# Placing VectorE sums one by one behind residual additions, and a score tile of its own for the last remainder product

## The chip, the cores and the metric

One core of a Trainium2 chip. The metric is the device time of one execution in microseconds (us), median of several runs. Five engines work side by side: TensorE (PE in the profile, PEld for its weight loads), VectorE (DVE), ScalarE (ACT), GpSimd (POOL) and SyncE (SP).

## The reference, cut to what matters

An attention with a relative bias for 8 batches of 576 tokens and 8 heads of 64, then a mixer: a low-rank product over the tokens with a residual, and a two-layer network with a residual.

```python
scores = scale * (q @ k.T) + bias            # per batch and head
x = softmax(scores) @ v                      # -> [8, 576, 512]
h = x.transpose(0, 2, 1) @ U @ V             # U [576, 32], V [32, 576]
u = x + h.transpose(0, 2, 1)
out = u + maximum(u @ w_ch1, 0.0) @ w_ch2    # w_ch1 [512, 2048], w_ch2 [2048, 512]
```

## The kernel before

The network's rows are handled in nine chunks of 512 rows: chunks 0 to 7 are the first 512 tokens of each batch, chunk 8 ("the last chunk", the remainder) the last 64 tokens of all batches. Chunks 7 and 8 are computed as a pair, with sums of their transposed tokens (fold_u), and the second matrix product of a chunk is cut into 2 x 2 blocks with seven products in place of eight. This takes sums of "inner rows" beforehand (low_sum, high_sums, last_sum) and additions of partial results afterwards (add with the residual u, and more). All of these sums and additions run on VectorE, in one queue.

This is the second product, with the cuts marked. `x`, `z` and `y` are three accumulators, each one PSUM bank; each `product` is 16 matmuls of 128 x 256 on TensorE. `y_first` is true for chunk 7 only, and only chunk 7 passes a `between` that does something: it places the sums for chunk 8.

```python
        x = bank()
        yield from product(x, "a11", "b11", True)
        add(x, blk(0, 0), u_of(j, 0, 0))
        z = bank()
        yield from product(z, "s3", "t3", True)
        add(z, blk(1, 1), u_of(j, 1, 1))
        if y_first:
            y = bank()
            yield from product(y, "a12", "b21", True)
            more(y, 0, 0)
        yield from product(x, "s2", "t2")
        add(x, blk(1, 0), u_of(j, 1, 0))
        for i in range(2):
            rows.last_sum(i)
        yield from product(z, "a22", "t4")
        more(z, 1, 0)
        between()
        yield from product(x, "s1", "t1")
        more(x, 1, 1)
        store(j, 1, ob[1])
        between()
        # ... (other chunks do product y here; chunk 8 does half of it)
        between()
        yield from product(x, "s2", "b22")
        add(x, blk(0, 1), u_of(j, 0, 1))
        # ... (stores)
```

A product may write into an accumulator again only after the addition behind the product before it has read the accumulator. This is the end of the program, where the last pair of heads is mixed while chunk 6's second product runs; PE takes chunk 6's matmuls between these calls, and all the rest after `work.finish()`:

```python
    work.run(0.5)
    hm = ps_s.tile([128, 2, 512], FP32, name="sc")
    mix_h(g, hm[:, 0, :])              # 4 matmuls, then addition u_tok on VectorE
    mix_rem(g, hm[:, 1, 0:128])()      # 1 matmul, then addition u_rem on VectorE
    fold_u(1, slice(0, 2))             # the four sums of transposed tokens
    for i in (2, 3, 4):
        fold_u(i, slice(0, 1))
    ready[B - 1] = ready[B] = True
    work.finish()
```

The softmax here doesn't subtract the row's maximum and nothing guards it: scores larger than these inputs give would overflow.

Of the kernel before, what the change touches and what calls it, by code (L numbers as in the profile page):

```python
# [12 lines left out]
FP32 = mybir.dt.float32  # L13
# [23 lines left out]
def kernel(  # L37
# [40 lines left out]
    ps_s = ctx.enter_context(  # L78
        tc.tile_pool(name="ps_s", bufs=2, space=bass.MemoryType.PSUM)
    )  # L80
# [343 lines left out]
    def add(ps, o, u):  # L424
        split = lambda x: x.rearrange("p t (a c) -> p t a c", c=128)
        nc.vector.tensor_tensor(out=split(o), in0=split(ps), in1=u, op=ALU.add)  # L426

    def u_of(j, i, h):
        t, a = slice(2 * i, 2 * i + 2), slice(2 * h, 2 * h + 2)
        if j < B:  # L430
            return u_tok[j % 3][:, a, t, :].rearrange("p a t c -> p t a c")
        return u_rem[:, t, a, :]
# [95 lines left out]
        yield from first_product(j, tail, g, sums)  # L528
        yield from second_product(j, rows)

    def second_product(j, rows, between=lambda: None, y_first=False):
        ob = [osb.tile([128, 2, DM], FP32, name="ob") for _ in range(2)]
        left = {
            "a11": lambda n: rows.lo[:, n, 0:256],
            "a12": lambda n: rows.hi[:, n, 0:256],
            "a22": lambda n: rows.hi[:, n, 256:512],
            "s1": lambda n: rows.s1[n // 4][:, n % 4, :],
            "s2": lambda n: rows.s2[n // 4][:, n % 4, :],
            "s3": lambda n: rows.s3[:, n, :],
        }  # L540
        right = {
            "b11": lambda n: w2b[:, n, 0:256],
            "b21": lambda n: w2b[:, 8 + n, 0:256],
            "b22": lambda n: w2b[:, 8 + n, 256:512],
            "t1": lambda n: tw[0][:, n, :],
            "t2": lambda n: tw[1][:, n, :],
            "t3": lambda n: w2b[:, n, 256:512],
            "t4": lambda n: tw[2][:, n, :],
        }

        def bank():
            return acc().rearrange("p (t c) -> p t c", t=2)

        def half(ps, a, b, t, first):
            for n in range(8):
                nc.tensor.matmul(  # L556
                    ps,
                    lhsT=left[a](n)[:, t * 128 : t * 128 + 128],
                    rhs=right[b](n),
                    start=first and n == 0,  # L560
                    stop=n == 7,
                    skip_group_check=True,
                )
                yield HALF

        def product(ps, a, b, first=False):
            for t in range(2):
                yield from half(ps[:, t, :], a, b, t, first and t == 0)

        def blk(i, h, t=slice(0, 2)):  # L570
            return ob[i][:, t, 256 * h : 256 * h + 256]

        def more(ps, i, h, t=slice(0, 2)):
            o = blk(i, h, t)
            nc.vector.tensor_tensor(out=o, in0=ps, in1=o, op=ALU.add)  # L575

        def late(t):
            y = acc()[:, 0:256].rearrange("p (t c) -> p t c", t=1)
            yield from half(y[:, 0, :], "a12", "b21", t, True)
            more(y, 0, 0, slice(t, t + 1))  # L580
            store_rem(0, ob[0], slice(t, t + 1), slice(0, 256))
# [6 lines that stand above are left out]
        add(z, blk(1, 1), u_of(j, 1, 1))  # L588
        if y_first:
            y = bank()  # L590
            yield from product(y, "a12", "b21", True)
            more(y, 0, 0)
        yield from product(x, "s2", "t2")
        add(x, blk(1, 0), u_of(j, 1, 0))
        for i in range(2):
            rows.last_sum(i)
        yield from product(z, "a22", "t4")
        more(z, 1, 0)
        between()
        yield from product(x, "s1", "t1")  # L600
        more(x, 1, 1)
        store(j, 1, ob[1])
        between()
        if j < B:
            if not y_first:
                y = bank()
                yield from product(y, "a12", "b21", True)
                more(y, 0, 0)
        else:
            store_rem(1, ob[1])  # L610
            yield from late(0)
        between()
        yield from product(x, "s2", "b22")
        add(x, blk(0, 1), u_of(j, 0, 1))
        if j < B:
            store(j, 0, ob[0])
        else:
            store_rem(0, ob[0], cols=slice(256, 512))
            yield from late(1)
# [25 lines left out]
    def fold_u(i, ks):  # L645
        o = slice(ks.start, ks.stop)
        b1, b2 = slice(ks.start, ks.stop), slice(2 + ks.start, 2 + ks.stop)
        t1, t2 = t12[:, b1, :], t12[:, b2, :]
        out_, x, y = (
            (t1, pb8[:, b1, :], pb7[:, b1, :]),  # L650
            (t2, pb8[:, b2, :], t1),
            (t34[:, b1, :], pb8[:, b2, :], pb8[:, b1, :]),
            (t34[:, b2, :], pb7[:, b2, :], t2),
        )[i - 1]
        nc.vector.tensor_tensor(out=out_, in0=x, in1=y, op=ALU.subtract)
# [8 lines left out]
    def pair_chunk(sixth):  # L664
# [5 lines left out]
        rows8 = Rows(  # L670
            *[t[:, 0:4096].rearrange("p (n c) -> p n c", c=S0) for t in flat],
            [], [],
            v_bf[0].rearrange("p k h c -> p (k h c)").bitcast(FP16)[
                :, 0:2048
            ].rearrange("p (n c) -> p n c", c=256),
        )
# [103 lines left out]
        todo8 = [lambda i=i: relu_act(rows8.hi[:, 2 * i : 2 * i + 2, :])  # L780
                 for i in range(4)]
        sums8 = [lambda i=i: rows8.low_sum(i) for i in range(2)]
        sums8 += [lambda i=i: rows8.high_sums(i) for i in range(2)]

        def between():
            while todo8:
                todo8.pop(0)()
            for _ in range(2):
                if sums8:
                    sums8.pop(0)()  # L790

        rest = second_product(B - 1, rows7, between, True)
        for p in range(67):
            if p in turns:
                f, n = turns[p]
# [297 lines left out]
    def mix_h(g, hm=None):  # L1093
        b, pr = divmod(g, NPAIR)
        x, tt = x_pr[g], tt_pr[g]
        if hm is None:
            hm = acc()
        for t in range(4):
            nc.tensor.matmul(  # L1099
                hm[:, t * 128 : (t + 1) * 128],  # L1100
                lhsT=vpad[:, t * 128 : (t + 1) * 128],
                rhs=tt,
                start=(t == 0),
                stop=(t == 3),
                skip_group_check=True,
            )
        nc.vector.tensor_tensor(  # L1107
            out=u_tok[b % 3][:, pr, :, :],
            in0=hm.rearrange("p (t c) -> p t c", t=4),
            in1=x[:, 0:4, :],  # L1110
            op=ALU.add,
        )
        if on_pe(g):
            return
        nc.sync.dma_start_transpose(
            out=uT[b % 3][:, pr, :].rearrange("c (t p) -> c t p", p=128),
            in_=u_tok[b % 3][:, pr, :, :].rearrange("p t c -> p (t c)"),
        )
# [23 lines left out]
    def mix_rem(g, hr):  # L1142
        b, pr = divmod(g, NPAIR)
        x, tt = x_pr[g], tt_pr[g]
        v0 = S0 - 64 if b % 2 else S0
        nc.tensor.matmul(hr, lhsT=vpad[:, v0 : v0 + 128], rhs=tt, start=True, stop=True)  # L1146
        rows = slice(64 * (b % 2), 64 * (b % 2) + 64)

        def post():
            nc.vector.tensor_tensor(  # L1150
                out=u_rem[rows, b // 2, pr, :],
                in0=hr[rows, :],
                in1=x[rows, 4, :],
                op=ALU.add,
            )
            if b % 2 == 0:
                return
            r = b // 2
            if b < B - 1:
                if pr < NPAIR - 1:  # L1160
                    return
                prs = slice(0, NPAIR)
            elif pr == 0:
                return
            else:
                prs = slice(0 if pr == 1 else pr, pr + 1)
            nc.sync.dma_start_transpose(
                out=uT_rem[:, prs, r * 128 : (r + 1) * 128],
                in_=u_rem[:, r, prs].rearrange("p a c -> p (a c)"),
            )  # L1170

        return post

    work = Work()
# [186 lines left out]
    for g in range(NPAIR, NG):  # L1361
        b, pr = divmod(g, NPAIR)
        for seg in range(3):
# [7 lines left out]
            if seg == 1:  # L1371
                n = 0
# [47 lines left out]
    def last_rem(g):  # L1420
        hr = ps_s.tile([128, 2, 512], FP32, name="sc")
        mix_rem(g, hr[:, 0, 0:128])()
# [14 lines left out]
    work.run(0.7)  # L1437
    turn(g)
    work.run(0.5)
    hm = ps_s.tile([128, 2, 512], FP32, name="sc")  # L1440
    mix_h(g, hm[:, 0, :])
    mix_rem(g, hm[:, 1, 0:128])()
    fold_u(1, slice(0, 2))
    for i in (2, 3, 4):
        fold_u(i, slice(0, 1))
    ready[B - 1] = ready[B] = True
# [31 lines left out]
```

## Time and profile before

| | before |
|---|---|
| median of 3 runs | 395.13 us (395.12 to 395.38) |
| profiled execution | 394.26 us, span 392.5 us |
| PE busy | 374.7 us, 95% of the span |
| VectorE busy | 313.0 us, 80% |
| waits of PE after 326 us | 0.78, 0.99 and 0.89 us |

The order of reading is: which engine is full, in which stretch it is not, and what the engine waited for in that stretch. From 326 us on PE is full but for the three waits, so they are all that a change of VectorE's order can win there. One thing about sizes: the profile models the end of a matmul, so an idle time of PE starts late. Of the wait before 373.95 us the profile shows 0.89 us, but the group before it started at 371.15 us and 16 matmuls take 1.745 us of PE's stream, so PE could have gone on at 372.90 us: 1.05 us. The difference, 0.16 to 0.17 us here and at the other waits, is what the profile adds to the last matmul of a group (1.91 - 1.745 us). The Trainium skill, "TensorE: Matmul & The Clock Gate", Single matmul latency, gives a single warm matmul (398 + N)/2.4 ns, 166 ns more than its N columns; the profile's ends agree with that, but since they are modelled this is no measurement of the array. I therefore compare starts.

### The profile page before, as it was taken

How to read it: one execution, taken by the hardware profiler on the slowest of the kernel's cores; microseconds unless marked ns; L12 is line 12 of the kernel's file. 1: busy time of each engine (PE TensorE's matmuls, PEld its weight loads, DVE VectorE, ACT ScalarE, POOL GpSimd, SP SyncE). 2: the span in 40 equal slices, each digit the busy share in tenths (PEclk: the TensorE clock that was granted, in tenths of full speed). 3: DMA queues.
4: the chain of work that ended last, by engine and by line, in shares of the span. 5: the costliest groups of instructions: out<-in, count | busy, mean ns of one | idle time of the engine just before them, and what ended most of it. 6: DMA issues, size and time to landing. Idle time of an engine off the chain costs nothing.

```text
span 392.5 us, 10256 instructions
## 1 busy us (share of the span) xinstructions
PE 374.7 (95%) x4145; PEld 249.4 (64%) x4145; DVE 313.0 (80%) x692; ACT 222.6 (57%) x338; POOL 129.0 (33%) x187
## 2 busy tenths in 40 slices
PE   7799999999999999999999999999999998999995
PEld 6366555565578656875588556865587467645874
DVE  7866898879898678878787788888997788678873
ACT  5987555555655676556655665556456650488400
POOL 4999817553454055405540543131000000000000
PEclk9999999999999999999999999999999999999999
DMA  7999999999999799959998999979003001200023
GB/s 135 170 106 170 166 203 109 165 72 183 154 74 107 161 126 90 81 145 139 111 70 134 134 126 68 92 182 133 17 16 116 21 8 35 109 0 2 0 109 107
DMA packets 163542, 40.66 MB, mean 104 GB/s; under 512 B 151632, under 2 KB 159096, under 8 KB 163496
## 3 DMA queue, kind: packets, MB, share of 16 engines
q0 software_dynamic: 110304, 18.24, 65.9%
q1 hardware_dynamic: 51928, 20.86, 25.2%
q10 hardware_dynamic: 1264, 0.92, 1.0%
q8 instruction: 32, 0.52, 0.6%
q14 instruction: 14, 0.11, 0.1%
HBM read 37.84 MB, written 9.45 MB: 120 GB/s over the span
## 4 chain that ended last, share of the span: by engine, by line
PE 84%; DVE 11%; ACT 2%; issue 1%; POOL 0%; DVEq 0%; POOLq 0%; ACTq 0%
PE acc L556 24%; PE acc L410 22%; PE o L1025 11%; PE sc L931 8%; PE acc L696 4%; PE acc L462 3%; DVE g L421 2%; PE sc L696 2%; PE acc L1099 2%; PE sc L949 2%; PE sc L970 1%; DVE p_sb L1001 1%; PE o L1183 1%; PE acc L905 1%; DVE qkT L874 1%
## 5 line engine op out<-in xcount | busy, mean ns | idle before, releaser
L940 ACT ACTIVATE p_sb<-sc 128x1024 bf16<-128x1024 f32 (+1 forms) x125 | 120.2, 1015 | 95.0 <-PE sc L931 95.0
L410 PE MATMUL acc<-uT,w1b 128*128 128x512 f16 x448 | 106.6, 380 | 1.2 <-ACT g L419 0.7
L410 PEld LDWEIGHTS <-w1b 128*128 128x128 f16 x448 | 40.5, 98 | 53.8 <-issue 13.9
L1001 DVE TENSOR_TENSOR p_sb<-p_sb,eb 128x768 bf16<-128x768 bf16 (+4 forms) x156 | 65.6, 454 | 0.6 <-ACT p_sb L940 0.4
L421 DVE TENSOR_SCALAR g<-acc 128x512 f16<-128x512 f32 x78 | 52.2, 684 | 7.9 <-PE acc L410 6.8
L1025 PEld LDWEIGHTS <-p_sb 128*128 128x128 bf16 x1550 | 53.4, 97 | 4.7 <-issue 0.9
L1025 PE MATMUL o<-v_bf,p_sb 128*128 128x65 bf16 x1475 | 55.6, 193 | 0.2 <-DVE xp L1051 0.2
L931 PE MATMUL sc<-qkT 64*128 64x512 bf16 x256 | 40.2, 382 | 1.5 <-ACT p_sb L940 0.9
L1381 POOL COPY gate<-xp 1x2 bf16<-1x2 bf16 x18 | 3.5, 193 | 112.7 <-DVE xp L1051 112.7
L556 PEld LDWEIGHTS <-g 128*128 128x128 f16 x336 | 32.1, 98 | 10.3 <-issue 5.4
L556 PEld LDWEIGHTS <-stage 128*128 128x128 f16 x336 | 32.1, 98 | 7.6 <-issue 3.4
L1051 DVE TENSOR_TENSOR xp<-o,rcp 128x320 bf16<-128x320 f32 x60 | 29.5, 492 | 3.2
L556 PE MATMUL acc<-w2b,g 128*128 128x256 f16 x224 | 28.1, 273 | 0.6 <-DVE g L421 0.6
L275 POOL DMA_DIRECT2D v_bf<-in_v_dram x32 | 28.5, 917 | 0.4 <-issue 0.3
L556 PE MATMUL acc<-tw,stage 128*128 128x256 f16 x224 | 28.1, 273 | 0.0
L419 ACT ACTIVATE g<-acc 128x512 f16<-128x512 f32 x34 | 20.4, 599 | 11.0 <-PE acc L410 10.8
L426 DVE TENSOR_TENSOR ob<-acc,u_tok 128x512 f32<-128x512 f32 x28 | 19.2, 688 | 9.2 <-PE acc L556 8.8
L1107 DVE TENSOR_TENSOR u_tok<-acc,xp 128x512 f16<-128x512 f32 x31 | 21.3, 687 | 6.2 <-PE acc L1099 6.0
L575 DVE TENSOR_TENSOR ob<-acc,ob 128x512 f32<-128x512 f32 (+1 forms) x25 | 16.7, 666 | 9.2 <-PE acc L556 8.9
L981 ACT ACTIVATE p_sb<-sc 128x640 bf16<-128x640 f32 x31 | 21.6, 698 | 0.3 <-PE sc L973 0.3
L962 ACT ACTIVATE p_sb<-sc 128x512 bf16<-128x512 f32 x31 | 18.5, 597 | 4.6 <-PE sc L1146 1.0
L275 POOL DMA_DIRECT2D qb<-in_k_dram x20 | 18.2, 910 | 1.6 <-issue 1.6
(168 smaller groups left out, 571.0 us busy)
## 6 DMA issues: line engine op xcount, KB each, us to landing
out_dram<-ob SPq DMA_DIRECT2D x16, 512.0 KB, 3.3
v_bf<-in_v_dram POOLq DMA_DIRECT2D x32, 128.0 KB, 5.9
qb<-in_q_dram POOLq DMA_DIRECT2D x23, 128.0 KB, 4.1
qb<-in_k_dram POOLq DMA_DIRECT2D x23, 128.0 KB, 4.2
w1b<-in_moe_w_ch_dram POOLq DMA_DIRECT2D x4, 512.0 KB, 6.6
w2b<-in_moe_w_ch_dram POOLq DMA_DIRECT2D x2, 1024.0 KB, 14.3
qb<-in_q_dram POOLq DMA_DIRECT2D x10, 64.0 KB, 5.3
qb<-in_k_dram POOLq DMA_DIRECT2D x10, 64.0 KB, 4.2
```

What stands on the lines that cost most here:

```text
L275: nc.gpsimd.dma_start(out=dst, in_=src[b, :, t * 128 : (t + 1) * 128, :].rearrange("h p d -> p h d"),)
L410: nc.tensor.matmul(gp_, lhsT=w1b[:, ct, nt * 128 : (nt + 1) * 128], rhs=rhs[:, ct, :], start=(ct == 0), stop=(ct == 3),)
L421: nc.vector.tensor_relu(out=g[:, nt, :], in_=gp_)
L556: nc.tensor.matmul(ps, lhsT=left[a](n)[:, t * 128 : t * 128 + 128], rhs=right[b](n), start=first and n == 0, stop=n == 7, skip_group_check ...
L696: nc.tensor.matmul(ps, lhsT=lhs, rhs=rhs[:, kt, :], start=first and kt == 0, stop=kt == 1, skip_group_check=True,)
L931: nc.tensor.matmul(sp[:, hh, :], lhsT=kT[rows, i * 128 : (i + 1) * 128], rhs=qT[rows, 0:S0], start=True, stop=True,)
L940: nc.scalar.activation(P[:, i, hh, 0:S0], sp[:, hh, :], AF.Exp, scale=scale)
L981: nc.scalar.activation(P4[:, 0:SP], sp.rearrange("p a c -> p (a c)")[:, 0:SP], AF.Exp, scale=scale,)
L1001: nc.vector.tensor_tensor(out=t, in0=t, in1=e, op=ALU.mult)
L1025: nc.tensor.matmul(o[:, qt * 66 : qt * 66 + 65], lhsT=lhs[:, c0 : c0 + 128], rhs=rhs, start=(kt == NKT and qt == 0), stop=(kt == NKT - 1), ...
L1051: nc.vector.tensor_tensor(out=xo[:, :, hh], in0=o[:, :, 0:64], in1=rbc, op=ALU.mult)
L1107: nc.vector.tensor_tensor(out=u_tok[b % 3][:, pr, :, :], in0=hm.rearrange("p (t c) -> p t c", t=4), in1=x[:, 0:4, :], op=ALU.add,)
```

## The change

The intent was to take all three waits of PE. The remainder product of the last pair of heads gets its own score tile; the token sums go behind residual additions of chunk 6; the sums of chunk 8's inner rows are placed one by one between chunk 7's additions instead of two (or four) at a time.

```diff
--- before.py
+++ after.py
@@ -528,7 +528,7 @@
         yield from first_product(j, tail, g, sums)
         yield from second_product(j, rows)
 
-    def second_product(j, rows, between=lambda: None, y_first=False):
+    def second_product(j, rows, between=lambda n: None, y_first=False):
         ob = [osb.tile([128, 2, DM], FP32, name="ob") for _ in range(2)]
         left = {
             "a11": lambda n: rows.lo[:, n, 0:256],
@@ -588,19 +588,21 @@
         add(z, blk(1, 1), u_of(j, 1, 1))
         if y_first:
             y = bank()
+            between(1)
             yield from product(y, "a12", "b21", True)
             more(y, 0, 0)
+            between(1)
         yield from product(x, "s2", "t2")
         add(x, blk(1, 0), u_of(j, 1, 0))
         for i in range(2):
             rows.last_sum(i)
         yield from product(z, "a22", "t4")
         more(z, 1, 0)
-        between()
+        between(1)
         yield from product(x, "s1", "t1")
         more(x, 1, 1)
         store(j, 1, ob[1])
-        between()
+        between(1)
         if j < B:
             if not y_first:
                 y = bank()
@@ -609,9 +611,9 @@
         else:
             store_rem(1, ob[1])
             yield from late(0)
-        between()
         yield from product(x, "s2", "b22")
         add(x, blk(0, 1), u_of(j, 0, 1))
+        between(6)
         if j < B:
             store(j, 0, ob[0])
         else:
@@ -780,12 +782,13 @@
         todo8 = [lambda i=i: relu_act(rows8.hi[:, 2 * i : 2 * i + 2, :])
                  for i in range(4)]
         sums8 = [lambda i=i: rows8.low_sum(i) for i in range(2)]
-        sums8 += [lambda i=i: rows8.high_sums(i) for i in range(2)]
-
-        def between():
+        sums8 += [lambda i=i, w=w: rows8.high_sums(i, (w,))
+                  for i in range(2) for w in range(2)]
+
+        def between(n):
             while todo8:
                 todo8.pop(0)()
-            for _ in range(2):
+            for _ in range(n):
                 if sums8:
                     sums8.pop(0)()
 
@@ -1437,10 +1440,11 @@
     work.run(0.7)
     turn(g)
     work.run(0.5)
-    hm = ps_s.tile([128, 2, 512], FP32, name="sc")
-    mix_h(g, hm[:, 0, :])
-    mix_rem(g, hm[:, 1, 0:128])()
+    mix_h(g, ps_s.tile([128, 2, 512], FP32, name="sc")[:, 0, :])
+    last_rem(g)
+    work.run(2.5)
     fold_u(1, slice(0, 2))
+    work.run(1.7)
     for i in (2, 3, 4):
         fold_u(i, slice(0, 1))
     ready[B - 1] = ready[B] = True
```

## The prediction

> **What bounds the kernel now.** I read the page first, then a table of busy times by stretch of the end of the run, because the compiled instruction streams of the two kernels agree on every engine until about 327 us: the matrix stream (PE) has the same 8292 rows in the same order and differs only in one output tile; ScalarE, GpSimd and SyncE keep their order; VectorE has the same operations, of which fourteen move. Nothing before 327 us can change.
>
> ```profile
> PE 374.7 (95%) x4145; PEld 249.4 (64%) x4145; DVE 313.0 (80%) x692; ACT 222.6 (57%) x338; POOL 129.0 (33%) x187
> ```
>
> PE is busy 95%. It is the bound, so only a gap of PE is worth anything. The table by stretch (columns: stretch, length, then PE, PEld, DVE, ACT, POOL busy, clock, DMA) says where gaps are:
>
> ```profile
> 326.90:331.00 4.10, 2.32 (x21) 1.90 (x20) 3.61 (x8) 0.00 (x0) 0.00 (x0) 1.00 0.18 40
> 331.00:336.10 5.10, 5.10 (x48) 4.56 (x48) 3.04 (x5) 0.00 (x0) 0.00 (x0) 1.00 0.01 3
> 336.10:361.10 25.00, 24.96 (x124) 11.97 (x123) 19.71 (x33) 18.43 (x32) 0.00 (x0) 1.00 0.11 43
> 361.10:373.90 12.80, 11.96 (x103) 9.97 (x102) 10.63 (x19) 5.92 (x7) 0.00 (x0) 1.00 0.00 0
> 373.90:388.20 14.30, 14.20 (x128) 12.41 (x127) 8.87 (x15) 0.00 (x0) 0.00 (x0) 1.00 0.30 99
> ```
>
> After 326.9 PE is short by 4.10 - 2.32 = 1.78 us in the first stretch and 12.80 - 11.96 = 0.84 us in the fourth; elsewhere it is full. The timeline of PE and of VectorE names both gaps (columns: start, duration, engine, line, operation, count, idle before and its releaser):
>
> ```profile
> 326.56 0.39 PE L1099 MATMUL sc<-tt,vpad 128*128 128x128 bf16 x4
> 327.73 0.22 PE L1146 MATMUL sc<-tt,vpad 128*128 128x128 bf16 x1 [0.78 <-DVE u_tok L1107]
> 328.00 1.91 PE L556 MATMUL acc<-tw,stage 128*128 128x256 f16 x16
> 330.91 1.91 PE L556 MATMUL acc<-tw,g 128*128 128x256 f16 x16 [0.99 <-DVE ob L426]
> ...
> 326.99 0.69 DVE L1107 TENSOR_TENSOR u_tok<-sc,xp 128x512 f16<-128x512 f32 x1 [0.91 <-PE sc L1099]
> 327.98 0.29 DVE L1150 TENSOR_TENSOR u_rem<-sc,xp 64x128 f16<-64x128 f32 x1 [0.31 <-PE sc L1146]
> 328.31 1.15 DVE L655 TENSOR_TENSOR uT<-uT_rem,uT 128x1024 f16<-128x1024 f16 x2
> 330.16 1.29 DVE L426 TENSOR_TENSOR ob<-acc,u_tok 128x512 f32<-128x512 f32 x2
> ```
>
> Gap A, 0.78 us: the remainder product (L1146) shares a score tile with the main mixing product (L1099) and waits until VectorE has read that one. Gap B, 0.99 us: the product that overwrites accumulator z waits for the residual addition z (L426 at 330.16), which stands in VectorE's queue behind the four sums of transposed tokens (L655). Gap C, 0.89 us, is in the second product of chunk 7:
>
> ```profile
> 372.01 1.28 DVE L491 TENSOR_TENSOR v_bf<-p_sb 128x1024 f16<-128x1024 f16 x2
> 373.21 0.68 DVE L575 TENSOR_TENSOR ob<-acc,ob 128x512 f32<-128x512 f32 x1
> 373.95 1.91 PE L556 MATMUL acc<-w2b,qkT 128*128 128x256 f16 x16 [0.89 <-DVE ob L575]
> ```
>
> The matmul at 373.95 may write accumulator x only once the addition at 373.21 has read it, and that came after two sums of the last chunk's rows.
>
> **What the skill says.** Trainium skill, "PSUM — Partial Sum Buffer", PSUM bank collisions raise a hardware error: guard PSUM by bank, not by address. The code's tile is 128 x 2 x 512 FP32, two banks, and the two products lie in different ones; so gap A is the tile-wise dependency, not a bank in use, and a separate tile may remove it. Same page, Engine vs sequencer instructions: VectorE's queue is strict first in, first out. The trace agrees: L426 at 330.16 runs behind L655 although its matmuls were done long before. Trainium skill, "VectorE: DVE Perf Modes", The perf-mode tier table: a two-tensor operation has a 2x mode for 16-bit SBUF operands, 1x with PSUM. The trace agrees: 128x1024 f16 in SBUF and 128x512 from PSUM both take about 0.69 us, so every moved sum costs as much as an addition.
>
> **Part 1, own score tile.** PE's four mixing matmuls are 0.055 us apart (0.22 us in the chain of waits), so the remainder product can start at 326.56 + 0.22 = 326.78, the last two z matmuls at 326.84 and 326.95, and the 16 of x (s2 by t2) at 327.06 instead of 328.00: 0.94 us.
>
> **Part 2, token sums behind the additions.** From 327.06 the 16 matmuls, 1.745 us (334.40 - 332.65, 0.109 each), end their turn at 328.80. They are followed by the z product, which needs addition z. VectorE: u_tok 326.99 to 327.68, u_rem from 327.70, addition z from 328.03 to 328.72, released 0.06 us later: 328.78. So PE is just not held, and starts at 328.80 instead of 330.91: 2.11 us won so far, 0.94 of it from part 1.
>
> Then I follow the moved sums, since they only change place. Addition x waits for its matmuls (a 16-matmul group ends 1.91 us after its start): 329.01. Two row sums, 0.60 apart, from 329.62; first token sum 330.9 to 331.6; "more z" 331.6 to 332.3; three token sums 0.34 apart, 332.28 to 333.38; "more x" 333.41 to 334.10. PE meanwhile runs s1 by t1 from 330.55, y from 332.29, and at 334.03 wants x again: a **new wait** of about 0.13 us, to 334.16. In the kernel before this matmul started at 336.14. Net of parts 1 and 2: 336.14 - 334.16 = 1.98 us.
>
> **Part 3, inner rows' sums one by one.** After: addition z 367.07, low sum 367.67, "more y" 368.28, low sum 368.88, addition x 369.60 (bound by its matmuls, as before), two row sums to 371.5, "more z" 371.41, one high sum 372.01 to 372.69. VectorE is then free when s1 by t1 ends, 371.15 + 1.91 = 373.06. "More x" starts at 373.10 instead of 373.21. PE follows 0.74 us after that start, as before (373.95 - 373.21): 373.84. **Gain 0.11 us, not 0.89**: the addition itself depends on the matmuls right before it, and product y that could fill the time has been moved ahead (y_first). The last three high sums then end near 377.7, and PE needs them at about 379.1; no new wait. The last store of chunk 7 is issued 0.7 us earlier, which only eases the output buffer's wait at 380.06, hidden anyway.
>
> Sum: 1.98 + 0.11 = 2.09 us. From 331 us PE is full apart from gap C, so an earlier start passes to the end; the final additions and stores shift with it. Predicted: 395.13 - 2.09 = **393.0 us**, 0.53%.
>
> **Rivals.** (1) *The backlog moves into the next wait*: sums postponed on VectorE hold "more x" longer than 0.13 us. For it: VectorE is busy 3.61 of 4.10 us in that stretch, and "more x" has no slack in my count. Against it: VectorE idled over 2 us between 332.65 and 336.34 in the kernel before. Each 0.1 us of error in a VectorE spacing shows fully; at worst half of B comes back, 393.6. (2) *Gap C closes wholly*, giving 0.78 us more: 392.3. For it speaks the order of the queue; against it the dependency just shown: 0.68 us of addition plus 0.10 of hand-over cannot overlap. (3) *Transposes bound*: the transposes of chunk 7 by SyncE (issued at 327.70 and 329.00) become the wait when PE arrives 2 us earlier. The median from issue to landing is 3.3 and 2.8 us, so they land near 331.0 and 331.8, needed at 334.3 and 335: hidden. If not, up to 1 us is lost: 394. (4) *Nothing*: hidden behind other work. Against it: PE has no other bound in those 61 us.
>
> **Range and chances.** The spread of the before-times is 0.26 us. Rival 1 or 3 gives up to 394, rival 2 down to 392.3. Range 392.5 to 393.9. The total of all three gaps is 2.66 us or 0.7%, so faster by over 2% is ruled out, and slower by 2% would need 8 us of new waits.
>
> **What would show it.** Right: no wait of L1146's counterpart on u_tok; PE's first matmul on z after the token products without a wait on L426's; first s2-by-b22 matmul of chunk 6 with a wait near 0.1 us on "more x"; the same matmul of chunk 7 still with 0.7 to 0.8 us of wait; span near 390.4. Wrong: a wait above 0.3 us on "more x" in chunk 6, one on a transpose at the first pair products, or a chunk-7 wait near zero.

## The result, and the profile after

The changed kernel took 392.70 us (392.12 to 393.53, 4 runs) against 395.12 us (394.30 to 395.38, 4 runs). The ratio is 0.9944, 95% interval 0.9917 to 0.9971, so it is faster, clear of the noise. A ratio here is the mean time of one kernel's runs over that of the other's of the same rounds, so not quite the ratio of the medians.

Line numbers of the changed kernel are 2 or 3 higher after the edit: L1102, L1149, L1110, L1153, L657 and L698 are L1099, L1146, L1107, L1150, L655 and L696 of before. First the table of busy times by stretch of the changed kernel, with the stretches cut at the first mixing matmul, at the first matmul of s2 by b22 in chunk 6 and in chunk 7, and at the last addition (columns as in the prediction):

```profile
327.77:335.25 7.48, 7.48 (x73) 6.73 (x71) 6.38 (x12) 0.00 (x0) 0.00 (x0) 1.00 0.11 24
335.25:372.95 37.70, 36.88 (x226) 21.91 (x224) 30.99 (x52) 24.36 (x39) 0.00 (x0) 1.00 0.08 28
372.95:387.19 14.24, 14.20 (x128) 12.42 (x127) 8.12 (x13) 0.00 (x0) 0.00 (x0) 1.00 0.31 99
```

PE is now full in the first stretch (7.48 of 7.48 us); what is left is in the second, 0.82 us. The timeline of PE in the changed kernel shows both places:

```profile
327.77 0.39 PE L1102 MATMUL sc<-tt,vpad 128*128 128x128 bf16 x4
327.99 0.22 PE L1149 MATMUL sc<-tt,vpad 128*128 128x128 bf16 x1
328.26 1.91 PE L556 MATMUL acc<-tw,stage 128*128 128x256 f16 x16
330.01 1.91 PE L556 MATMUL acc<-tw,g 128*128 128x256 f16 x16
335.25 0.27 PE L556 MATMUL acc<-w2b,stage 128*128 128x256 f16 x1
...
370.26 1.91 PE L556 MATMUL acc<-tw,qkT 128*128 128x256 f16 x16
372.95 1.91 PE L556 MATMUL acc<-w2b,qkT 128*128 128x256 f16 x16 [0.78 <-DVE ob L575]
```

The remainder product (L1149) starts 0.22 us after the mixing product, the product on z (330.01) waits for nothing, and so does the first s2-by-b22 matmul of chunk 6 (335.25). The same matmul of chunk 7 still waits 0.78 us, where it was 0.89. VectorE's timeline of the changed kernel says why:

```profile
329.24 0.69 DVE L426 TENSOR_TENSOR ob<-acc,u_tok 128x512 f32<-128x512 f32 x1
332.02 0.68 DVE L657 TENSOR_TENSOR uT<-uT_rem,uT 128x1024 f16<-128x1024 f16 x1
334.23 0.68 DVE L575 TENSOR_TENSOR ob<-acc,ob 128x512 f32<-128x512 f32 x1
...
371.12 0.68 DVE L503 TENSOR_TENSOR stage<-p_sb,p_sb 128x1024 f16<-128x1024 f16 x1
372.21 0.69 DVE L575 TENSOR_TENSOR ob<-acc,ob 128x512 f32<-128x512 f32 x1 [0.40 <-PE acc L556]
```

Addition z (329.24) now comes before the first token sum (332.02). "More x" of chunk 6 ends at 334.91 us, 0.34 us before PE needs it. In chunk 7, VectorE was free and waited 0.40 us for PE before "more x" (372.21): the wait is no longer VectorE's queue, but the addition itself.

The time comes from three stretches, measured between starts:

| | before | after |
|---|---|---|
| A: first mixing matmul to first s2-by-b22 matmul, chunk 6 | 9.58 | 7.48 |
| B: start of s1 by t1 to start of s2 by b22, chunk 7 | 2.80 | 2.69 |
| C: first mixing matmul to start of the last VectorE addition | 61.63 | 59.42 |

So 2.10 + 0.11 = 2.21 us were won in all. The spans of the two profiled executions differ by only 1.0 us, because the profiled execution of the changed kernel reached the first mixing matmul 1.21 us later (327.77 against 326.56), in code that the change doesn't touch. This is the row from 15 to 25 us of the table by stretch of the changed kernel, and then of the kernel before (the third number from the right is the granted clock):

```profile
15.00:25.00 10.00, 8.12 (x104) 5.22 (x104) 7.18 (x21) 8.60 (x12) 9.35 (x15) 0.83 1.60 132
```

```profile
15.00:25.00 10.00, 8.03 (x135) 5.36 (x132) 6.88 (x21) 9.19 (x13) 9.35 (x15) 1.00 1.69 137
```

The clock fell to a mean of 0.83 in one and not in the other, at nearly the same busy time of PE. The traces of the experiments fit this: the four with 0.83 in this row (the changed kernel twice, e1_tile, e5b_split) reach the first mixing matmul at 327.54 to 327.77 us, the six with 1.00 and no late weights (see e2_late) at 326.25 to 327.00 us. It does not go by the code: e5_split and e5b_split are one program, with 1.00 and with 0.83. Executions of the kernel before seem to fall into it too: of eleven runs, the three with a granted clock of 0.996 took 395.37 to 395.65 us, the eight with 0.998 or more 393.86 to 395.28 us. It is not the only thing that varies: in another call one of its runs took 395.67 us at 0.999. That is why the experiments below are read from stretches A, B and C, and the totals only as a check.

### The profile page after: what moved, and what is told of

Its sections match the earlier page's. It is cut to its first block, busy times and chain, and to the rows that moved or that the text cites. A ratio compares the mean times of both kernels' runs of the same rounds, so it can differ in the third digit from the quotient of the medians.

```text
span 391.5 us, 10253 instructions
## 1 busy us (share of the span) xinstructions
PE 375.2 (96%) x4142; PEld 249.8 (64%) x4145; DVE 312.7 (80%) x692; ACT 222.7 (57%) x338; POOL 129.4 (33%) x187
## 4 chain that ended last, share of the span: by engine, by line
PE 85%; DVE 9%; ACT 3%; DMA 1%; issue 1%; SPq 0%; ACTq 0%; DVEq 0%
PE acc L556 26%; PE acc L410 22%; PE o L1028 11%; PE sc L934 8%; PE acc L698 4%; PE acc L462 3%; DVE g L421 2%; PE sc L698 2%; PE acc L1102 2%; PE sc L952 2%; DVE p_sb L1004 1%; PE sc L973 1%; PE acc L908 1%; DMA stage<-in_q_dram 1%; DVE qkT L877 1%; PE o L698 1%
## 5 line engine op out<-in xcount | busy, mean ns | idle before, releaser
L1028 PEld LDWEIGHTS <-p_sb 128*128 128x128 bf16 x1550 | 54.3, 98 | 5.0 <-issue 1.3
L1110 DVE TENSOR_TENSOR u_tok<-acc,xp 128x512 f16<-128x512 f32 x31 | 21.3, 688 | 6.2 <-PE acc L1102 6.0
```

The source lines that it names most:

```text
L1028: nc.tensor.matmul(o[:, qt * 66 : qt * 66 + 65], lhsT=lhs[:, c0 : c0 + 128], rhs=rhs, start=(kt == NKT and qt == 0), stop=(kt == NKT - 1), ...
L1110: nc.vector.tensor_tensor(out=u_tok[b % 3][:, pr, :, :], in0=hm.rearrange("p (t c) -> p t c", t=4), in1=x[:, 0:4, :], op=ALU.add,)
```

## The experiments

All outputs are right. Kernels are compared only within the same rounds. The kernel before: 394.26 us for e1 to e4, 394.39 us for e0_after, e5_split, e6 and e7, 394.75 us for e5b_split and e8 (medians of 11).

| run | A | B | C | median | ratio to before, 95% interval |
|---|---|---|---|---|---|
| kernel before | 9.58 | 2.80 | 61.63 | | |
| e1_tile: own tile alone | 9.31 | 2.81 | 61.36 | 395.11 | 1.002 (0.9995 to 1.0045) |
| e2_late: token sums alone | 8.43 | 2.80 | 60.48 | 394.29 | 0.999 (0.9974 to 1.0006) |
| e3_tile_late: both | 7.48 | 2.80 | 59.53 | 392.96 | 0.996 (0.9945 to 0.9975) |
| e4_inner: inner sums alone | 9.58 | 2.69 | 61.52 | 394.63 | 1.001 (0.9992 to 1.0027) |
| e0_after: changed kernel again | 7.49 | 2.69 | 59.43 | 392.06 | 0.9943 (0.9924 to 0.9962) |
| e6_double: one token sum twice | 7.92 | 2.69 | 59.86 | 393.51 | 0.9965 (0.9943 to 0.9987) |
| e5_split: y cut in two | 7.49 | 2.70 | 58.55 | 391.41 | 0.9926 (0.9906 to 0.9945) |
| e5b_split: the same again | 7.48 | 2.69 | 58.55 | 392.17 | 0.9931 (0.9910 to 0.9953) |
| e7_split_pairs: y cut, sums in pairs | 7.48 | 2.80 | 59.14 | 392.28 | 0.9943 (0.9924 to 0.9962) |
| e8_add_first: two of four sums behind the addition | 7.48 | 2.80 | 58.66 | 391.16 | 0.9914 (0.9896 to 0.9933) |

In the last four rows B holds half of product y, 0.87 us of matmuls.

### e1_tile: part 1 alone

```diff
-    hm = ps_s.tile([128, 2, 512], FP32, name="sc")
-    mix_h(g, hm[:, 0, :])
-    mix_rem(g, hm[:, 1, 0:128])()
+    mix_h(g, ps_s.tile([128, 2, 512], FP32, name="sc")[:, 0, :])
+    last_rem(g)
```

> Kernel before with part 1 alone (own score tile for the remainder product; token sums still ahead of addition z, inner sums as before). I measure from the first of the four mixing matmuls (time 0) to the first s2-by-b22 matmul of chunk 6: 9.58 us before, 7.48 after. My theory: the VectorE queue decides, so freeing the tile only lets u_rem and all behind it run 0.28 us earlier; PE's wait at the remainder product vanishes but the wait before the z product grows from 0.99 to about 1.66 us of idle; stretch 9.30 us, total 0.3 us faster. Rival (each gap is worth what its wait shows): stretch 8.64 us, total 0.9 us faster.

The timeline of PE in this kernel:

```profile
327.76 0.22 PE L1146 MATMUL sc<-tt,vpad 128*128 128x128 bf16 x1
331.61 1.91 PE L556 MATMUL acc<-tw,g 128*128 128x256 f16 x16 [1.66 <-DVE ob L426]
```

The wait at the remainder product is gone, and the wait before the product on z grew from 0.99 to 1.66 us, as expected. A is 9.31 us: of the 0.94 us that PE wins at the first wait it keeps 0.27, the time by which u_rem and all behind it in VectorE's queue start earlier. The rival, 8.64 us, is out. The total does not show the 0.27 us; its runs reach from 393.73 to 397.46 us.

### e2_late: part 2 alone

```diff
     fold_u(1, slice(0, 2))
+    work.run(1.7)
     for i in (2, 3, 4):
```

and `work.run(2.5)` ahead of the first token sum; the shared tile stays.

> Kernel before with part 2 alone (token sums behind the residual additions; score tile shared as before). My theory: the wait of 0.78 us at the remainder product stays, the z product no longer waits; stretch from first mixing matmul to first s2-by-b22 matmul 8.43 us, total 1.15 us faster. Together with part 1 alone (0.28) this gives 1.43, less than the 2.10 of both, because the two waits are in series on VectorE. Rival (parts simply add): 2.10 - 0.28 = 1.82 us, stretch 7.76.

The timeline of PE in this kernel:

```profile
329.98 0.22 PE L1146 MATMUL sc<-tt,vpad 128*128 128x128 bf16 x1 [0.78 <-DVE u_tok L1107]
332.00 1.91 PE L556 MATMUL acc<-tw,g 128*128 128x256 f16 x16
```

A is 8.43 us, the number expected. So part 1 alone is worth 0.27 us, part 2 alone 1.15 us, and both 2.10 us: 0.68 us more than their sum. The two waits lie one behind the other, and the time is handed on in one direction only. Part 2 alone wins its whole wait (1.16 us by starts: 330.91 - 328.00 - 1.745). Part 1 alone hands 0.67 of its 0.94 us to the wait behind it, and is worth 2.10 - 1.15 = 0.95 us only once part 2 is there.

The median of the total, 394.29 us, shows no gain against 394.26 us, and the interval just misses the 0.9971 that 1.15 us would be. The profiled execution reached the first mixing matmul only at 328.81 us. Its list of PE's waits before 326 us has a first line that the kernel before has not:

```profile
PE acc L410 <- DMA w1b<-in_moe_w_ch_dram: 1.7, 1, 1.7
```

The first layer's weights came late, 1.7 us of wait for a load that is the same in all these kernels (e6_double shows 1.1 us of it). With this and the clock, the part of the run that no edit touches took from 326.25 to 328.81 us in the traces here. The totals of e1, e2 and e4 are therefore inconclusive; whether their edits also change how often the early part is slow is left open.

### e3_tile_late and e4_inner: parts 1 and 2, and part 3 alone

e3_tile_late takes both edits above; e4_inner takes the diff's edits to `between`, `second_product` and `sums8` alone.

> Parts 1 and 2 without part 3. My theory: stretch 7.48 us as in the changed kernel, no wait of PE in it; chunk 7's wait on 'more x' stays at 0.89 us of idle (2.80 us from the start of s1-by-t1 to the start of s2-by-b22); total 2.10 us faster than before, so part 3 is worth 0.1. Rival (part 3 matters more, because the sums left in pairs also hold later additions): well above 0.3 us slower than the changed kernel.

> Part 3 alone. My theory: stretch of chunk 6 stays at 9.58 us; from s1-by-t1 to s2-by-b22 in chunk 7 2.69 us instead of 2.80; total 0.11 us faster, inside the noise. Rival: the sums placed one by one remove the wait of chunk 7, 1.75 us there and 0.9 to 1.05 us in total.

In e3_tile_late A is 7.48 us without a wait, and chunk 7's wait is that of the kernel before. PE's timeline, e3_tile_late and then e4_inner:

```profile
372.29 1.91 PE L556 MATMUL acc<-w2b,qkT 128*128 128x256 f16 x16 [0.89 <-DVE ob L575]
```

```profile
373.70 1.91 PE L556 MATMUL acc<-w2b,qkT 128*128 128x256 f16 x16 [0.78 <-DVE ob L575]
```

Part 3 alone moves 0.89 to 0.78 us and C by 0.11 us (61.63 to 61.52; with the other parts by 0.10, 59.53 to 59.43). Both rivals are out. The repeat of the changed kernel, e0_after, gave the same stretches within 0.01 us:

> The changed kernel again, as the base of this call. By its first trace: stretch from first mixing matmul to first s2-by-b22 matmul of chunk 6 7.48 us, s1-by-t1 to s2-by-b22 of chunk 7 2.69 us, 2.2 us faster than the kernel before. If the start, where the granted clock can fall, varies again, the stretches repeat to 0.05 us while the total varies by over 1 us.

### e6_double: is "more x" of chunk 6 close to PE's path?

The prediction had a new wait of 0.13 us there, the trace has none. One token sum is done twice, with the same result, ahead of the three later ones.

```diff
     work.run(1.7)
+    fold_u(1, slice(0, 2))
     for i in (2, 3, 4):
```

> The changed kernel with the first token sum (128x1024 f16, 0.60 us of VectorE's queue) done a second time, with the same result, just before the three later ones. My trace shows 'more x' ended 0.34 us before PE needs it. If this queue is what the prediction's new wait of 0.13 us depended on, the slack turns into a wait: stretch 7.48 + 0.32 = 7.80 us, with PE waiting for 'more x'. Rival (the slack is larger than the trace suggests, VectorE not on the path): stretch stays 7.48 us.

The timeline of VectorE, and then of PE, in this kernel:

```profile
332.99 1.15 DVE L657 TENSOR_TENSOR uT<-uT_rem,uT 128x1024 f16<-128x1024 f16 x2
334.73 1.28 DVE L575 TENSOR_TENSOR ob<-acc,ob 128x512 f32<-128x512 f32 x2
```

```profile
335.46 0.27 PE L556 MATMUL acc<-w2b,stage 128*128 128x256 f16 x1 [0.28 <-DVE ob L575]
```

PE now waits for "more x", and A is 7.92 us, 0.43 more than in e0_after; 0.32 had been expected. From the start of "more z" (its lines are not shown) to that of "more x" VectorE took 334.73 - 332.39 = 2.34 us against 334.23 - 332.62 = 1.61 us in the changed kernel, so the doubled sum cost 0.73 us, not 0.60, because the sum behind it reads its result and starts only after its end. 0.73 - 0.43 leaves 0.30 us of slack, which agrees with the trace of the changed kernel: "more x" ends at 334.91, PE follows 0.05 to 0.06 us after such an end, and needs it at 335.25, 0.28 us. The queue is what decides there, and the slack is small.

### e5_split: covering the addition with other matmuls

If the rest of chunk 7's wait is an addition that nothing covers, other matmuls between s1 by t1 and s2 by b22 must take it. Half of product y is free to stand there.

```diff
             y = bank()
             between(1)
-            yield from product(y, "a12", "b21", True)
-            more(y, 0, 0)
+            yield from half(y[:, 0, :], "a12", "b21", 0, True)
             between(1)
 ...
             if not y_first:
                 y = bank()
                 yield from product(y, "a12", "b21", True)
-                more(y, 0, 0)
+            else:
+                yield from half(y[:, 1, :], "a12", "b21", 1, False)
+            more(y, 0, 0)
```

> The changed kernel, and product y of chunk 7 cut in two: its first half (8 matmuls, 0.87 us) stays before s2-by-t2, its second half goes between s1-by-t1 and s2-by-b22. My theory: the wait on 'more x' is an addition of 0.68 us and its hand-over that nothing covers; 0.87 us of other matmuls cover it, so 2.69 us become 2.69 with the half product inside, wait under 0.15 us, 0.8 to 0.87 us faster than the changed kernel. Rival (VectorE is too full there; the additions come later as PE comes earlier, or s2-by-t2 now waits for its row sum): a new wait of 0.3 us or more and under 0.5 us of gain.

> The changed kernel with product y cut in two, once more, as base of this call. From the first mixing matmul to the start of the last VectorE addition its first trace took 58.55 us (changed kernel 59.42, kernel before 61.63). Theory: 58.55 us again within 0.05, and about 0.8% faster than the kernel before, whatever the start of the run adds.

The timeline of PE in e5_split:

```profile
368.15 1.91 PE L556 MATMUL acc<-tw,qkT 128*128 128x256 f16 x16
369.90 1.04 PE L556 MATMUL acc<-w2b,g 128*128 128x256 f16 x8
370.85 1.91 PE L556 MATMUL acc<-w2b,qkT 128*128 128x256 f16 x16
```

B is still 2.70 us, but the half product is inside it: the eight matmuls from 369.90 last 0.87 us of PE's stream, to 370.77, and PE goes on at 370.85. The wait that is left is 0.08 us, too short to show as idle. C is 58.55 us, 0.88 us less than in the changed kernel's repeat, and 58.55 again in e5b_split. By medians this version is 391.41 us against 392.06 us of the changed kernel and 394.39 us of the kernel before. Its runs overlap with those of the changed kernel (391.05 to 392.62 and 391.81 to 393.21 us), so that step is shown by C and not by the totals.

### e7_split_pairs and e8_add_first: what part 3 is worth once the addition is covered

e7_split_pairs keeps parts 1 and 2 and cuts y in two, but places the inner sums as the kernel before does (low sums as a pair before "more x", all four high sums behind it).

> As the run with y cut in two, but the inner sums placed in pairs as in the kernel before. My theory: once other matmuls cover 'more x', part 3 is worth at most 0.1 us: wait before s2-by-b22 below 0.25 us, total within 0.15 us of the run with y cut in two. Rival (with less time in all, the pairs hold up the additions): 0.3 us or more slower than it.

B is 2.80 us, 0.10 us of it from the pair of low sums, as expected. But C is 59.14 us, 0.59 more than in e5_split: the rival was right. The timeline of VectorE, then of PE, in e7_split_pairs:

```profile
370.53 0.68 DVE L503 TENSOR_TENSOR stage<-p_sb,p_sb 128x1024 f16<-128x1024 f16 x1
371.25 0.69 DVE L503 TENSOR_TENSOR stage<-stage,p_sb 128x1024 f16<-128x1024 f16 x1
371.86 0.69 DVE L503 TENSOR_TENSOR stage<-p_sb,p_sb 128x1024 f16<-128x1024 f16 x1
373.79 0.68 DVE L426 TENSOR_TENSOR ob<-acc,u_tok 128x512 f32<-128x512 f32 x1
377.39 1.29 DVE L426 TENSOR_TENSOR ob<-acc,u_rem 128x512 f32<-128x512 f32 x2 [2.32 <-DMA out_dram<-ob]
```

```profile
378.13 1.91 PE L556 MATMUL acc<-tw,p_sb 128*128 128x256 f16 x16 [0.31 <-DVE ob L426]
```

The four sums hold back "more y" and the last addition of chunk 7 (373.79, though its matmuls started at 370.67 and end 1.91 us later). The store waits for that addition, and chunk 8's addition z (377.39) waits for the store, since it needs the store's buffer (the pool of output tiles has two); PE then waits for that addition. By starts this is 378.13 - 375.91 - 1.745 = 0.47 us, and with the 0.10 us it makes the 0.59.

e8_add_first tests this chain: as e7_split_pairs, but two of the four high sums are placed behind the last addition.

```diff
-        between()
         yield from product(x, "s2", "b22")
         add(x, blk(0, 1), u_of(j, 0, 1))
+        between()
 ...
-            for _ in range(2):
+            for _ in range(2 if len(sums8) > 2 else 1):
```

> As the run with y cut in two and inner sums in pairs, but only two of the four high sums stand before the last addition of chunk 7 and two behind it (the low sums still as a pair before 'more x'). In the run with all four before it, that addition, the store behind it and chunk 8's addition z, which needs the store's buffer, came late and PE waited 0.31 us. My theory: with two moved behind, this wait is gone and the stretch is 58.65 us (the 0.10 us of the pair before 'more x' stays). Rival (the wait has another cause, such as the two sums that remain, or a slower store): the wait at chunk 8's z product stays at 0.3 us and the stretch near 59.14 us.

The timeline of VectorE, then of PE, in e8_add_first:

```profile
373.32 0.69 DVE L426 TENSOR_TENSOR ob<-acc,u_tok 128x512 f32<-128x512 f32 x1
377.35 0.69 DVE L426 TENSOR_TENSOR ob<-acc,u_rem 128x512 f32<-128x512 f32 x1 [1.41 <-DMA out_dram<-ob]
```

```profile
378.36 1.91 PE L556 MATMUL acc<-tw,p_sb 128*128 128x256 f16 x16
```

The last addition starts right behind its matmuls (371.38 + 1.91 = 373.29), the store's landing still ends VectorE's wait, but PE no longer waits. C is 58.66 us, where 58.65 was expected. Its median of 391.16 us is the lowest of all; against e5b_split (392.17 us) the stretch is 0.11 us longer, so the totals do not rank the two; in the profiled pair the early part of the run differs, with the first mixing matmul at 326.96 and 327.70 us.

## Why the prediction was right

The time, 392.70 us, lies in the range, 0.3 us under the 393.0 told. That the total came so near is partly luck: the four runs reach from 392.12 to 393.53 us, and the same kernel again (e0_after) had a median of 392.06 us, below the told range of 392.5 to 393.9, with the same A, B and C within 0.01 us. The span told, 390.4 us, was 391.5 in the profiled execution, whose early part was slow, and 390.3 to 391.8 over the four runs. What the mechanism is judged by is A, B and C: 2.09 us told, 2.21 measured. Step by step:

- **Only the end of the run changes, and PE bounds it: right.** In the changed kernel the stretches sum to the gain, 2.10 + 0.11 us. One detail does not come out: by the order of VectorE's operations in the two traces nine sums change place among the others (four token sums, two low and three high sums), not fourteen; how these were counted, and the 8292 rows of PE, is not on record.
- **Part 1, the wait is the tile's and not the bank's: right.** With a separate tile the remainder product starts 0.22 us after the mixing product. The 0.94 us counted for it hold only together with part 2 (0.95 us); alone it is worth 0.27 us, as e1_tile shows.
- **Part 2, addition z just in time: right.** Predicted 2.11 us up to the product on z (from 330.91 to 328.80); measured, from the first mixing matmul, 330.91 - 326.56 = 4.35 us before and 330.01 - 327.77 = 2.24 us after, 2.11.
- **The new wait of 0.13 us on "more x": wrong.** There is none, and 0.28 us of slack. The step that failed is the chain of starts behind the moved sums: "first token sum 330.9 to 331.6; 'more z' 331.6 to 332.3 ... 'more x' 333.41 to 334.10". Counted from the first mixing matmul it puts "more x" at 6.85 us; the trace has 334.23 - 327.77 = 6.46. I added whole durations of 0.7 us in some places, where VectorE starts an operation that doesn't need the one before 0.60 to 0.61 us after it. In all that is 0.39 us too late, of which only the told wait of 0.13 us reached PE's path. This accounts for the difference between 2.09 us predicted and 2.21 measured; e6_double shows that the queue itself was rightly seen as close to PE's path.
- **Part 3 worth 0.11 us, not 0.89: right**, by e4_inner and by e3_tile_late against the changed kernel. The reason told, an addition and its hand-over that nothing covers, is shown by e5_split: covering them takes 0.88 us.
- **"Every moved sum costs as much as an addition": wrong as it stands.** It holds for the sums of 128x1024 (0.68 us); the three later token sums are 128x512 and took 0.42 us (the prediction's own chain has them 0.34 apart). A slip: the 393.6 of rival 1 should read 393.5 (393.04 + 0.50).
- **The store is "hidden anyway": right for this kernel only.** e7_split_pairs shows it costing 0.47 us once PE runs earlier and four sums stand ahead of the addition; in e5_split, with PE as early and the sums one by one, it costs nothing.
- **Transposes hidden: right.** No wait of PE or VectorE on them shows in the changed kernel after 326 us.

## What to carry to other kernels

When two waits of the bounding engine lie one behind the other on the same in-order queue, taking the first alone can hand most of its gain to the second (0.27 of 0.94 us kept here; the second alone 1.15, both 2.10); judge edits to such a queue as a set. A wait for an addition that reads the product just finished is not cured by clearing the queue ahead of it (0.11 us), but by other matmuls in between (0.88 us). And when PE moves forward, look again at what was hidden: a sum placed ahead of the addition that frees a store can become the next wait.

## What the Trainium skill lacked or had wrong

- "VectorE: DVE Perf Modes", The DRAIN you can't avoid: it reports for eight copies that a semaphore after each costs nothing extra. An operation that reads the result of the one before starts 0.72 us after it (370.53 to 371.25), one that doesn't 0.61 us after it (371.25 to 371.86), same size and type. The page gives no figure for a dependent pair, and both the prediction's wrong step and the 0.73 us in place of 0.60 in e6_double turn on it.
- "Perfetto Trace Analysis", Per-instruction lifecycle: what the profiler-reported window actually captures: it names the propagation of a semaphore between engines, and that page gives no time for it from VectorE to TensorE. Here the matmul that waits for an addition starts 0.05 us after the addition's end (0.052 to 0.053 in the unrounded times, at every such wait after 326 us in all twelve traces; 0.05 and 0.06 by the rounded lines, 372.21 + 0.69 to 372.95 and 373.21 + 0.68 to 373.95).
